# RWKV-7 attention feeding a SoLU expert on one core: carrying the products with r as 64 more columns through carry, drive and solve, and placing full-array runs between runs of 64x64 groups

## The chip, the core and the metric

The kernel runs on one core of one Trainium2 chip. The metric is device time in microseconds for one execution of the whole program, everything from the inputs in DRAM to the output in DRAM. The kernel before the change took 622.96 us (median of three runs: 614.93, 622.96, 625.33). Everything is computed in fp32.

## The reference, cut to what matters

Two blocks follow each other. The first is a recurrence over 768 time steps for 4 batches x 8 heads, each with a 40x40 state; its output of 3072 tokens x 320 goes into the second, a feed-forward block with a softmax-weighted activation (SoLU), a normalisation and a second matrix.

```
state = 0                                           # B=4, H=8, D=40 x D=40
for t in range(768):
    y[:, :, t] = einsum('bhd,bhde->bhe', r_t, state)
    Sa = einsum('bhde,bhe->bhd', state, a_t)
    state = state * w_t[:, :, None, :] - einsum('bhd,bhe->bhde', Sa, b_t)
    state = state + einsum('bhd,bhe->bhde', v_t, k_t)

x = y.transpose(0, 2, 1, 3).reshape(3072, 320)
h = x @ w_in                                        # 320 -> 1024
e = exp(h - max(h));  solu = h * e / (sum(e) + 1e-9)
mu = mean(solu);  var = mean((solu - mu) ** 2)
out = ((solu - mu) / sqrt(var + 1e-6) * g_ln) @ w_out   # 1024 -> 320
```

`moe_w_in`, `moe_w_out` arrive as 64-bit floats (seen as int64) and are narrowed to fp32 on the chip during the first iterations.

## The kernel before, in words

**Chunks.** Time is cut into chunks of 64 steps (C). Two batches are handled together, so there are 24 units of work i = 0..23: pair `bp = i % 2` and chunk `ci = i // 2` (`where_`, L285). Within a chunk the recurrence becomes a few matrix products and the inverse of a unit lower triangular 64x64 matrix per head, here 16 heads of 64 at a time (two batches x eight heads). A unit `(p, q, g, h)` (L257) is one batch p and one head 4q+2g+h. The products of 64x64 (or 40x64) use the tensor engine as four tiles of 64x64, and `in_turn` (L259) orders 16 of them so that the four tiles take turns. Such a group of 16 products is called a group here. All of them go through `mm` (L267), so the profile shows them at L268. Products of the second block use the full 128x128 array.

**Pieces of one iteration.** The main loop (L835 to L905) runs i from -1 to 27. One iteration works on four chunks at once: on chunk i (solve, read out), on i+1 (couple, carry, drive), on i+5 (`j = i + AHEAD`; the keys, `norm`, the inverse) and on m-2 = i-3 and m-3 = i-4 (the second block). In the order of the tensor engine before the change:

- `solved(i)` (L576): 16 products into `pu`, 64 columns (`x0` by `tu`, giving `nuT`, the transposed solution), and 16 into the same buffer with 40 columns (`lu`'s right part). ScalarE copies both out, negated.
- `scores(i+1)` (L530): two groups into `ps`, masked on VectorE into `psi` and the left 64 columns of `lv`. `lv` holds per head 64 columns of masked v-by-r products and 40 columns of v.
- transposes: `stated(i)`, `front(j)`, `front_b(j)`, `decay_turned(j+1)`, eight of them each (`turned`, L350); evicted to `s`, `aT`, `bT`, `ex`.
- `hidden(m-2)` (L673): the second half of `h = x @ w_in` as full-array products with 512 columns (two with 64 rows, two full), with `decay(j+2)`'s product `pcum` between.
- `norm(j)` (L406): one group into `pnt`; ScalarE copies it into `nt`, and POOL writes `nt` to DRAM.
- `answered(i)` (L595): one group into `pl`, `nuT` by `rT`; VectorE masks it into the left 64 columns of `lu`.
- `carried(i+1)` (L548): one group into `px`, `aT` by the state, 40 columns.
- `read(i, True)` (L606): into `pyo`, first `s` by `rT` (64 columns, the state times r), then half of the products `kb` by `lv` and `kb` by `lu` with 104 columns (64 of output, 40 of new state).
- `output(m-3)` (L738): eight full-array products `lnT` by `w2` into `po`, evicted by ScalarE as `osb` (scaled by `rs`) and written out by a DMA on ScalarE's queue.
- `fence` (L272, a drain of the tensor engine), `couple(i+1)` (L479) into `py`, `read(i, False)`, the other half of `pyo`, `driven(i+1)` (L564), the second part of `px`, 40 columns, evicted to `x0`, and `close(i+1)` (L492) into `pz`, evicted into `tu`.
- `leave(i)` (L630): VectorE multiplies the left 64 columns of `pyo` by the decays `ex` into `x`, and SP writes `x` to `xT` by DMA; VectorE adds the right 40 to the state into `tot`, and POOL multiplies by `ex` into the state `st`.
- `attend_r(i+2)` (`pr`), `folded(m-2)` (16 transposes of `e` into `plnT`), `attend_kv(i+2)` (`pkv`), and `hidden(m-1)`, the first two products of the next `h`.

**Other engines.** ScalarE (ACT) does the exponentials, most evictions and, in `spreadof` (L709), the squares for the variance with an accumulator. VectorE (DVE) does the masks, `nmax` (the row maxima of `h`, L690), `weighed` (L700, `e` times `h`) and the inverse. POOL scales keys (`scaled`, L341), multiplies the state, takes the power for `rs`, and issues some DMAs. SP issues most DMAs, in program order.

**The inverse.** The diagonal 32x32 blocks of two chunks together (`GRP` = 2) are inverted on VectorE by `invert` (L435): `nt` is gathered from DRAM into `blk`, then 30 steps of a product (`prod`, L448) and a subtraction (`uu`, L450) follow. The generator is advanced by `some(n)` and `narrow(...)`; `pieces` (L837) says how many steps stand at each place of an iteration: (5, 2, 2, 5) in odd iterations, (6, 2, 2, 6) in even ones. The result goes to DRAM (`uu_dram`, L456, on SP), is read back as `tu` and `uh` by `bring` (L460) at the start of the iterations that come next, and `flip` (L473) transposes `tu`'s blocks on VectorE ahead of `couple`.

**What sets the order.** The kernel is scheduled by hand: each engine executes in the order of the program text, and semaphores are put in where data or buffers demand it. On-chip buffers for matrix products are shared by tag ("A", "B", "C" and "h", each of two banks, one buffer per tag), so a new tile of a tag waits for the readers of the last.

Of the kernel before, what the change touches and what calls it, by code (L numbers as in the profile page):

```python
# [17 lines left out]
P = 128  # L18
C = 64
# [31 lines left out]
def kernel(  # L51
# [32 lines left out]
    small = ctx.enter_context(tc.tile_pool(name="small", bufs=4))  # L84
# [41 lines left out]
    st_t = zeroed(nc.vector, "st", [P, 8, C], NPAIR)  # L126
    tu_t = zeroed(nc.vector, "tu", [P, H, 3 * Q], 2)
    uh_t = zeroed(nc.vector, "uh", [P, 2 * H, Q], 2)
    x0 = zeroed(nc.vector, "x", [P, 2, 4, C], 1, lambda x: x[:, :, :, D:])[0]
# [264 lines left out]
    def masked(dst, t):  # L394
        nc.vector.tensor_tensor(out=dst, in0=t.rearrange("p b (j c) -> p b j c", j=4),  # L395
                                in1=tri.unsqueeze(1).unsqueeze(1).to_broadcast([P, 2, 4, C]), op=ALU.mult)
# [9 lines left out]
    def norm(i):  # L406
        if not ok(i):
            return
        d = st[i]
        t = pair("A", "pnt")  # L410
        for u in in_turn(lambda p, q, g, h: (h, p ^ h)):
            p, q, g, h = u
            j = 2 * q + g
            mm(t[half(p ^ h), h, j * C:j * C + C], keyed(d["bT"], u), keyed(d["aT"], u))
        nt = d["nt"] = tokens("nt", AHEAD)
        nc.scalar.copy(out=nt, in_=t[:, :, 0:256].rearrange("p b (j c) -> p b j c", j=4))  # L416
# [18 lines left out]
    def invert(n):  # L435
# [18 lines left out]
        for y in range(2):  # L454
            queue = nc.sync if n or not y else nc.scalar
            queue.dma_start(out=inverse[n][:, y::2], in_=u[C * y:C * y + C])  # L456
# [22 lines left out]
    def couple(i, tag):  # L479
        if not ok(i):  # L480
            return
        d = st[i]
        t = pair(tag, "py")
        for u in in_turn(lambda p, q, g, h: (p ^ h, p)):
            p, q, g, h = u
            j = 2 * q + g
            x = half(p ^ h)
            mm(t[half(p), h, j * Q:j * Q + Q], d["nt"][x, h, j], d["tu"][x, 4 * h + j, 0:Q])
        nc.scalar.activation(out=wy[:, :, :, 0:Q], in_=t[:, :, 0:4 * Q].rearrange("p h (j c) -> p h j c", j=4),
                             func=AF.Copy, scale=c_("neg_hi"))  # L490

    def close(i):  # L492
# [3 lines left out]
        t = pair("B", "pz")  # L496
        for u in in_turn(lambda p, q, g, h: (p, p ^ h)):
            p, q, g, h = u
            j = 2 * q + g
            mm(t[half(p ^ h), h, j * Q:j * Q + Q], wy[half(p), h, j], d["uh"][half(p), 2 * (4 * h + j) + (p ^ h)])  # L500
# [4 lines left out]
    def attend_kv(i):  # L505
        if not ok(i):
            return
        d = st[i]
        t = pair("B", "pkv")
        k, v = turned(t, 0, d["kb"]), turned(t, 1, v_t[0])  # L510
        d["kT"] = kept("kT", k)
        d["vT"] = kept("vT", v)

    def attend_r(i, tag):
        if not ok(i):
            return
        st[i]["rT"] = kept("rT", turned(pair(tag, "pr"), 0, r_t[0]), 2)

    def stated(i, t, y):
        if not ok(i):  # L520
            return lambda: None
        d = st[i]
        bp, ci = where_(i)
        if not ci:
            return lambda: None
        t = turned(t, y, st_t[bp])
        d["s"] = two.tile([P, 4, P], FP32, tag="s", name="s", bufs=1)
        return lambda: nc.scalar.copy(out=d["s"][0:W2].rearrange("p j (b t) -> p b j t", b=2), in_=t)

    def scores(i):  # L530
        if not ok(i):
            return
# [10 lines left out]
        psi = d["psi"] = tokens("psi", 2)  # L543
        masked(psi, t[:, :, 0:256])
        masked(d["lv"].rearrange("p (q x) c -> p q x c", q=2)[:, :, :, 0:C], t[:, :, 256:])


    def carried(i):  # L548
# [7 lines left out]
        if ci:  # L556
            for u in in_turn(lambda p, q, g, h: (h, p ^ h)):
                p, q, g, h = u
                j = 2 * q + g
                mm(d["px"][half(p ^ h), h, j * D:j * D + D], keyed(d["aT"], u),  # L560
                   st_t[bp][rows(h), 4 * p + 2 * g + q, 0:D], start=(h, p ^ h) not in d["opened"], stop=False)
                d["opened"].add((h, p ^ h))

    def driven(i):  # L564
# [3 lines left out]
        for u in in_turn(lambda p, q, g, h: (p, p ^ h)):  # L568
            p, q, g, h = u
            j = 2 * q + g  # L570
            mm(d["px"][half(p ^ h), h, j * D:j * D + D], d["psi"][half(p), h, j],
               d["lv"][half(p), head(u), C:W2], start=(h, p ^ h) not in d["opened"])
            d["opened"].add((h, p ^ h))
        nc.scalar.copy(out=x0[:, :, :, 0:D], in_=d["px"][:, :, 0:4 * D].rearrange("p h (j d) -> p h j d", j=4))

    def solved(i):  # L576
        if not ok(i):
# [3 lines left out]
        for u in in_turn(lambda p, q, g, h: (p ^ h, q)):  # L581
            p, q, g, h = u
            at, x = (2 * h + g) * C, half(p ^ h)
            mm(t[half(q), p ^ h ^ q, at:at + C], x0[x, h, 2 * q + g], d["tu"][x, 4 * h + 2 * q + g, Q:])
        for u in in_turn(lambda p, q, g, h: (p ^ h, p)):
            p, q, g, h = u
            at, x = 256 + (2 * q + g) * D, half(p ^ h)
            mm(t[half(p), h, at:at + D], d["tu"][x, 4 * h + 2 * q + g, Q:], x0[x, h, 2 * q + g, 0:D])
        nuT = d["nuT"] = tokens("nuT")
        lu = d["lu"] = two.tile([P, H, W2], FP32, tag="lu", name="lu", bufs=1)  # L590
        nc.scalar.mul(out=nuT[0:W2], in_=t[0:W2, :, 0:256].rearrange("p b (j c) -> p b j c", j=4), mul=-1.0)
        nc.scalar.mul(out=lu.rearrange("p (j h) c -> p h j c", h=2)[:, :, :, C:],
                      in_=t[:, :, 256:256 + 4 * D].rearrange("p h (j d) -> p h j d", j=4), mul=-1.0)

    def answered(i):  # L595
# [3 lines left out]
        t = pair("B", "pl")  # L599
        for u in in_turn(lambda p, q, g, h: (q, p)):  # L600
            p, q, g, h = u
            at = (2 * g + h) * C
            mm(t[half(p), q, at:at + C], d["nuT"][rows(q), p ^ h ^ q, 2 * h + g], valued(d["rT"], u))
        masked(d["lu"].rearrange("p (q x) c -> p q x c", q=2)[:, :, :, 0:C], t[:, :, 0:256])

    def read(i, own):  # L606
        if not ok(i):
            return
        d = st[i]
        bp, ci = where_(i)  # L610
        if own:
            d["po"] = pair("A", "pyo")
            d["opened"] = set()
            if ci:
# [321 lines left out]
```

## Time and profile before

| | us |
|---|---|
| three runs | 614.93, 622.96, 625.33 (median 622.96) |
| profiled execution, its own time | 621.36 |
| its span in the trace | 619.5 |
| PE matmuls busy (12,309 of them) | 518.1 |
| PE weight loads busy | 367.3 |
| DVE busy (1,119 instructions) | 404.5 |
| ACT busy (668) | 317.3 |
| POOL busy (441) | 261.6 |
| DVE, the inverse's `prod` and `uu` (720 instructions) | 209.7 |
| PE, `h<-w_in,xT` | 125.3 |
| PE, `po<-w,lnT` | 109.5 |
| 2% of the median | 12.5 |

Mean granted clock of the tensor engine: 0.915. The chain of work that ended last lies on PE for 63% of the span, on DVE for 17%, on "issue" for 8% (time in which the engine waited for nothing that the profile shows), on DMA for 5%, on ACT for 3%.

A row of a timeline reads: start in us from the start of the span, duration in us, engine, line of the code, operation, output tile and input tiles, shape, how many instructions are put together in the row (x8), and in brackets how long the engine stood idle before and what ended that. PEld is the loading of weights into the array, which overlaps PE. SPq, ACTq are DMA issues on the queues of SP and ACT.

### The profile page before, as it was taken

What the parts mean: (1) busy time and instruction counts of PE and PEld (TensorE: products, weight loads), DVE (VectorE), ACT (ScalarE), POOL (GpSimd) and SP (SyncE); (2) the same over time, 40 slices, a digit from 0 to 9 for tenths busy, and PEclk for the clock granted to TensorE, in tenths of its full rate; (3) what the DMA queues carried; (4) which work ended last, traced back from release to release, by engine and by line L of the source; (5) the groups of instructions that cost most, each with busy time, mean ns of one, the idle gap of its engine ahead of it and who ended that gap; (6) DMA issues with size and microseconds to landing.
All of it is one profiled execution on the core that took longest, in us unless ns stands there. A gap on an engine that the chain in (4) does not pass through costs nothing.

```text
span 619.5 us, 28385 instructions
## 1 busy us (share of the span) xinstructions
PE 518.1 (84%) x12309; PEld 367.3 (59%) x12309; DVE 404.5 (65%) x1119; ACT 317.3 (51%) x668; POOL 261.6 (42%) x441
## 2 busy tenths in 40 slices
PE   5443776887889989899889799989899898999993
PEld 3332665665667667666666566757666566756552
DVE  4695889888977858767766658578676575332230
ACT  4534455565556556565555355656554455544332
POOL 3362354275572555444714625625634433122200
PEclk9655656599999999999899989999999999999999
DMA  8986977557545554654654553655523432110100
GB/s 161 158 158 110 192 150 136 110 120 127 91 105 96 114 119 98 121 110 93 125 90 81 121 91 72 126 96 102 107 56 73 92 62 51 33 34 26 27 19 21
DMA packets 213907, 60.03 MB, mean 97 GB/s; under 512 B 199120, under 2 KB 208952, under 8 KB 213784
## 3 DMA queue, kind: packets, MB, share of 16 engines
q1 hardware_dynamic: 195512, 33.78, 33.2%
q0 software_dynamic: 11568, 19.78, 13.5%
q10 hardware_dynamic: 6704, 4.67, 2.8%
q8 instruction: 97, 1.59, 1.1%
q14 instruction: 26, 0.21, 0.1%
HBM read 40.10 MB, written 13.37 MB: 86 GB/s over the span
## 4 chain that ended last, share of the span: by engine, by line
PE 63%; DVE 17%; issue 8%; DMA 5%; ACT 3%; POOL 1%; SPq 0%; ACTq 0%; DVEq 0%; POOLq 0%
PE h L268 18%; PE po L745 12%; DVE uu L450 5%; PE pyo L268 5%; DVE prod L448 5%; PE pu L268 4%; PE ps L268 4%; PE px L268 3%; PE py L268 2%; PE plnT L731 2%; PE pst L355 2%; PE pcum L336 2%; PE pkv L355 2%; PE pz L268 2%; DMA blk<-nt_dram 2%
## 5 line engine op out<-in xcount | busy, mean ns | idle before, releaser
L268 PE MATMUL h<-w_in,xT 128*128 128x512 f32 (+1 forms) x288 | 125.3, 625 | 0.1
L448 DVE TENSOR_TENSOR prod<-blk,uu 128x30 f32<-128x30 f32 (+4 forms) x360 | 104.7, 291 | 29.7 <-DMA blk<-nt_dram 19.0
L450 DVE TENSOR_TENSOR uu<-uu,prod 128x30 f32<-128x30 f32 (+4 forms) x360 | 105.0, 292 | 12.4
L745 PE MATMUL po<-w,lnT 128*128 128x320 f32 x384 | 109.5, 438 | 1.8 <-ACT lnT L735 1.8
L745 PEld LDWEIGHTS po<-w,lnT 128*128 128x128 f32 x384 | 71.2, 190 | 32.6 <-ACT lnT L735 1.9
L268 PEld LDWEIGHTS h<-w_in,xT 128*128 128x128 f32 (+1 forms) x288 | 41.0, 191 | 43.0 <-issue 38.4
L690 DVE TENSOR_REDUCE nmax<-h 128x1 f32<-128x1024 f32 x24 | 29.4, 1224 | 47.3 <-PE h L268 47.3
L721 POOL TENSOR_TENSOR rs<-var,mhalf 128x1 f32<-128x1 f32 x24 | 13.5, 564 | 100.5 <-ACT var L720 99.9
L421 POOL DMA_DIRECT2D nt_dram<-nt x20 | 18.6, 930 | 85.8 <-ACT nt L416 51.7
L432 POOL DMA_DIRECT2D blk<-nt_dram x46 | 36.8, 806 | 30.1 <-DMA nt_dram<-nt 26.6
L670 POOL DMA_DIRECT2D xT<-x x96 | 48.6, 511 | 0.0
L639 DVE TENSOR_TENSOR x<-pyo,ex 104x256 f32<-104x256 f32 x48 | 18.1, 419 | 46.6 <-PE pyo L268 43.9
L658 POOL TENSOR_TENSOR st<-tot,ex 104x160 f32<-104x160 f32 x44 | 24.2, 567 | 51.3 <-DVE tot L654 51.0
L698 ACT ACTIVATE e<-h,nmax 128x1024 f32<-128x1024 f32 x24 | 26.7, 1114 | 32.1 <-DVE nmax L690 30.1
L336 PE MATMUL pcum<-lw,cst 128*128 128x320 f32 x48 | 23.5, 579 | 22.4 <-ACT lw L327 21.5
L719 ACT ACTIVATE h<-e,mu 128x1024 f32<-128x1024 f32 x24 | 26.8, 1118 | 19.8 <-DVE e L706 19.8
L395 DVE TENSOR_TENSOR psi<-ps,cst 128x512 f32<-128x512 f32 x24 | 16.5, 687 | 28.1 <-PE ps L268 27.9
L291 POOL DMA_DIRECT2D raw_r<-in_r_dram x48 | 34.1, 713 | 0.0
L747 ACT ACTIVATE osb<-po,rs 128x320 f32<-128x320 f32 x24 | 12.6, 525 | 41.6 <-PE po L745 39.9
L268 PE MATMUL pyo<-lu,kb 64*64 64x104 f32 x768 | 29.4, 262 | 5.4 <-DVE lu L395 3.1
L706 DVE SCALAR_TENSOR_TENSOR e<-h,e 128x1024 f32<-128x1024 f32 x24 | 29.3, 1219 | 5.8 <-ACT e L698 5.8
L268 PE MATMUL py<-tu,nt 64*64 64x32 f32 x768 | 17.7, 230 | 17.3 <-DVE tu L477 11.3
(136 smaller groups left out, 1101.1 us busy)
## 6 DMA issues: line engine op xcount, KB each, us to landing
blk<-nt_dram POOLq DMA_DIRECT2D x46, 128.0 KB, 4.6
nt_dram<-nt POOLq DMA_DIRECT2D x20, 256.0 KB, 3.8
raw_w<-in_w_dram SPq DMA_DIRECT2D x48, 80.0 KB
a<-in_a_dram SPq DMA_DIRECT2D x48, 80.0 KB
raw_r<-in_r_dram POOLq DMA_DIRECT2D x48, 80.0 KB, 4.0
lv<-in_v_dram SPq DMA_DIRECT2D x48, 80.0 KB
out_dram<-osb ACTq DMA_DIRECT2D x24, 160.0 KB
raw_b<-in_b_dram SPq DMA_DIRECT2D x44, 80.0 KB
```

The source lines that it names most:

```text
L268: nc.tensor.matmul(o, lhsT=lhsT, rhs=rhs, start=start, stop=stop, skip_group_check=True)
L291: queue.dma_start(out=x[half(p), :, 0:D], in_=ap[2 * bp + p, :, ci * C:(ci + 1) * C, :].rearrange("h t d -> t h d"))
L336: nc.tensor.matmul(t, lhsT=c_("cum"), rhs=d["lw"], start=True, stop=True)
L432: queue.dma_start(out=nb[home:home + Q], in_=blocks[n][:, Q * e:Q * e + Q, Q * e:Q * e + Q])
L448: nc.vector.tensor_tensor(out=t, in0=nb[:, j:j + 1, j + 1:Q].to_broadcast([P, n_c, m]), in1=u[:, 0:n_c, j:j + 1].to_broadcast([P, n_c, m]) ...
L450: nc.vector.tensor_tensor(out=u[:, 0:n_c, j + 1:Q], in0=u[:, 0:n_c, j + 1:Q], in1=t, op=ALU.subtract)
L670: nc.gpsimd.dma_start(out=xT[to:to + Q, 2], in_=x[at + P - 3 * D:at + D, 2])
L690: nc.vector.tensor_reduce(out=nmax, in_=d["h"], axis=AX.X, op=ALU.max, negate=True)
L698: nc.scalar.activation(out=e, in_=d["h"], func=AF.Exp, bias=d["nmax"], accum_out=d["esum"])
L706: nc.vector.scalar_tensor_tensor(out=d["e"], in0=d["h"], scalar=1.0 / DFF, in1=d["e"], op0=ALU.mult, op1=ALU.mult, accum_out=d["mu"])
L719: nc.scalar.activation(out=d["h"], in_=d["e"], func=AF.Square, scale=-float(DFF), bias=d["mu"], accum_out=sq)
L745: nc.tensor.matmul(t, lhsT=d["lnT"][:, f, :], rhs=w2[:, f, :], start=f == 0, stop=f == NF - 1)
```

## The change

It does the following.

- The state's tile `st` gets a second plane of 64 columns. A new group `stated_r(i+1)` makes the state times r first (`s` by `rT` into `psr`), and ScalarE puts it into plane 0; plane 1 is the state as before. `carried` then runs with both planes, 128 columns, `driven` with the 104 columns of `lv` (in place of its right 40), `x0` holds 104 columns per head, negated at its eviction, and `solved` makes one group with 104 columns in place of two. Its left 64 columns are masked straight from `pu` into `lu`. `nuT`, `answered` and the group `pl` are gone, and so is `pyo<-rT,s`: `leave` adds plane 0 to `pyo`'s left columns instead.
- `leave` adds both parts on VectorE into a `tot` of 104 columns, and the multiplication by the decays into `x` is on POOL (it was on VectorE).
- `read(i)` is one run, and it stands ahead of `output`, with `leave` behind it. `output` is in two halves of four products: one behind `read`, one behind `norm`.
- `couple` and `norm` share one buffer and follow each other; `norm` moves from behind `highest` to behind `couple`, so that the writing of `nt`, and on every second iteration the start of the next inverse, move too. The drain ahead of `couple` is gone. `flip` moves up to just behind `highest`, `spreadof` behind `norm`, `weighed` behind `leave`.
- `stated` now works for i+1, and the order and the buffers of the transposes change: `pst` takes `stated` and `front_b`, "A" takes `front` and `decay_turned`. `attend_kv` evicts with one copy for k and v, `folded` with one in place of two, and the evictions of the three are put behind all their transposes. `hidden` runs (2,0), (2,1) and then, behind the transposes, (0,1), (1,1) without `pcum` between.
- The inverse's steps per iteration: (0, 2, 2, 10) in odd iterations, (3, 2, 2, 9) in even ones.

```diff
-    st_t = zeroed(nc.vector, "st", [P, 8, C], NPAIR)
+    st_t = zeroed(nc.vector, "st", [P, 2, 8, C], NPAIR)
...
-    x0 = zeroed(nc.vector, "x", [P, 2, 4, C], 1, lambda x: x[:, :, :, D:])[0]
+    x0 = const.tile([P, 2, 4, W2], FP32, name="x0")
...
+    def stated_r(i):
...
+        t = pair("C", "psr")
+        for u in in_turn(lambda p, q, g, h: (q, h)):
+            p, q, g, h = u
+            at = (2 * p + g) * C
+            mm(t[half(h), q, at:at + C], d["s"][rows(q), 2 * p + g, h * C:h * C + C], valued(d["rT"], u))
+        nc.scalar.copy(out=state_of(i)[:, 0].rearrange("p (x q) c -> p q x c", q=2), in_=by_units(t[:, :, 0:256]))
...
-                mm(d["px"][half(p ^ h), h, j * D:j * D + D], keyed(d["aT"], u),
-                   st_t[bp][rows(h), 4 * p + 2 * g + q, 0:D], start=(h, p ^ h) not in d["opened"], stop=False)
+                mm(d["px"][half(p ^ h), h, j * P:j * P + P], keyed(d["aT"], u),
+                   state_of(i)[rows(h), :, 4 * p + 2 * g + q], start=(h, p ^ h) not in d["opened"], stop=False)
...
-            mm(d["px"][half(p ^ h), h, j * D:j * D + D], d["psi"][half(p), h, j],
-               d["lv"][half(p), head(u), C:W2], start=(h, p ^ h) not in d["opened"])
+            mm(d["px"][half(p ^ h), h, j * P:j * P + W2], d["psi"][half(p), h, j],
+               d["lv"][half(p), head(u)], start=(h, p ^ h) not in d["opened"])
...
-        nc.scalar.copy(out=x0[:, :, :, 0:D], in_=d["px"][:, :, 0:4 * D].rearrange("p h (j d) -> p h j d", j=4))
+        nc.scalar.mul(out=x0, in_=d["px"].rearrange("p h (j d) -> p h j d", j=4)[:, :, :, 0:W2], mul=-1.0)
...
-        for u in in_turn(lambda p, q, g, h: (p ^ h, q)):
-            p, q, g, h = u
-            at, x = (2 * h + g) * C, half(p ^ h)
-            mm(t[half(q), p ^ h ^ q, at:at + C], x0[x, h, 2 * q + g], d["tu"][x, 4 * h + 2 * q + g, Q:])
...
+            at, x = (2 * q + g) * W2, half(p ^ h)
+            mm(t[half(p), h, at:at + W2], d["tu"][x, 4 * p + 2 * q + g, Q:], x0[x, h, 2 * q + g])
...
+        nc.scalar.copy(out=o[:, :, :, C:], in_=y[:, :, :, C:])
+        masked(o[:, :, :, 0:C], y[:, :, :, 0:C])
...
-    def answered(i):
...
+            for x, part in enumerate((slice(0, C), slice(C, W2))):
+                nc.vector.tensor_tensor(out=by_b(tot)[:, :, :, part], in0=y[:, :, :, part],
+                                        in1=by_b(state_of(i)[:, x])[:, :, :, 0:part.stop - part.start], op=ALU.add)
...
-            nc.vector.tensor_tensor(out=x[0:W2, 2 * q:2 * q + 2].rearrange("p g (b t) -> p b g t", b=2),
-                                    in0=y[:, q, :, 0:C].rearrange("p (b g) c -> p b g c", b=2),
-                                    in1=ex[:, :, 2 * q:2 * q + 2, 0:C], op=ALU.mult)
+            nc.gpsimd.tensor_tensor(out=x[0:W2, 2 * q:2 * q + 2].rearrange("p g (b t) -> p b g t", b=2),
+                                    in0=by_q(tot, q)[:, :, :, 0:C], in1=ex[:, :, 2 * q:2 * q + 2, 0:C], op=ALU.mult)
...
-        pieces = shares.get(i, (5, 2, 2, 5) if i % GRP else (6, 2, 2, 6))
+        pieces = shares.get(i, (0, 2, 2, 10) if i % GRP else (3, 2, 2, 9))
```

The new order of the main loop, behind `solved(i)` and `scores(i+1)`:

```
hidden(m - 2, ((2, 0), (2, 1)))
tc_, ta = pair("C", "pst"), pair("A", "pa")
for evict in [stated(i + 1, tc_, 0), front_b(j, tc_, 1), front(j, ta, 0), mask_values, decay_turned(j + 1, ta, 1)]:
    evict()
hidden(m - 2, ((0, 1), (1, 1)))
decay(j + 2); stated_r(i + 1); narrow(some_weights[1], pieces[1])
highest(m - 2); flip(i + 1); scaled(j + 1); left(i - 1)
exped(m - 2); by_value(i + 2); read(i); some(pieces[2])
output(m - 3, 0); leave(i); weighed(m - 2); carried(i + 1)
coupled = couple(i + 1); norm(j, coupled)          # and begin_inverse in every second iteration
spreadof(m - 2); output(m - 3, 1); narrow(some_weights[2], pieces[3], ...)
close(i + 1); driven(i + 1)
keys_out, fold_out, r_out = attend_kv(i + 2), folded(m - 2), attend_r(i + 2, "C")
for evict in [fold_out, keys_out, r_out]:
    evict()
hidden(m - 1, ((0, 0), (1, 0)))
```

## The prediction, made before the changed kernel ran

> **What bounds the kernel now.** I read the page's busy shares first, then the clock and the instruction queue, then the timeline of the tensor engine through one iteration after another.
>
> ```profile
> PE 518.1 (84%) x12309; PEld 367.3 (59%) x12309; DVE 404.5 (65%) x1119; ACT 317.3 (51%) x668; POOL 261.6 (42%) x441
> ...
> PEclk9655656599999999999899989999999999999999
> ...
> q8 instruction: 97, 1.59, 1.1%
> ```
>
> The tensor engine (PE) is the busiest; its clock is full after the first fifth except for two dips. Queue q8 moved 97 packets of 1.59 MB in all, 16 KB each. PE's 24,618 loads and matmuls make 254 per packet. So q8 brings PE's own instructions, 256 at a time.
>
> I date iterations by the first matmul into `pu`: 160.26 us at i=4, 361.05 at i=13, 380.47 at i=14, 486.94 at i=19, 562.30 at i=23. From i=4 to 18 all work runs: 15 iterations of 21.78 us. But i=13 took 19.42, with no gap in it. The 2.36 us between are gaps of this kind:
>
> ```profile
> 219.79 0.39 PE L355 MATMUL pkv<-cst,kb 64*104 64x64 f32 x8
> 220.02 0.33 PE L355 MATMUL pkv<-cst,v 64*104 64x64 f32 x5
> 221.40 0.32 PE L355 MATMUL pkv<-cst,v 64*104 64x64 f32 x3 [1.06 <-issue]
> 221.65 1.98 PE L268 MATMUL h<-w_in,xT 128*128 128x512 f32 x4
> ```
>
> The engine stops inside a run of equal transposes and waits for nothing that a semaphore shows. Numbering PE's records from the first, every such stop from 160 us on stands behind number 256k+192, and a q8 packet comes just before it ends. At these boundaries PE loses 30.9 us from i=4 to 18, 3.7 us from i=19 to 22, and 5.7 us between 60 and 160 us. Two long stops (2.74 us at 303.1, 3.87 at 350.3) are followed by 3.4 and 6.8 us at half clock, where `h<-w_in` takes 3.40 in place of 1.98 us; worked from such rows that is 4.5 us more. Together 39.1 us after 160, on the path because nothing else holds PE there.
>
> When does a boundary stop PE? From one boundary to the first instruction behind the next, the stopped ones take 3.4 to 4.5 us (181.26 to 185.18, 258.78 to 263.24), three late ones 7.8 to 10.8. If the 256 instructions between take longer than that, nothing is lost. An fp32 product is two loads and two matmuls, so 16 products of 64x64 are 64 instructions in 0.44 to 0.52 us, while eight full-array products for `po` are 32 in 4.5 us. The dense run from `pnt` to the first `pyo` holds 320 instructions in 2.8 us, that from `py` to `pkv` 304 in 3.1: a block inside lasts about 2 us, and PE waits for the other two.
>
> **PE work, part by part, per iteration**, in start-to-start times. Out: `pu`'s groups of 64 and 40 columns (0.51+0.44), `pl` (0.46), the 40-column `px` groups (0.44 each), the drain in front of `py` (0.22): 2.51. In: `pu` with 104 columns and drive with 104 (16 products of 104 took 0.36+0.38 in `pyo`: 0.74 each), carry with 128 (0.74 x 128/104 = 0.91): 2.39. `psr` replaces `pyo<-rT,s` at 0.50. Turns between 64x64 and full-array work go from three each way to five: the last group ahead of such a run shows 0.46 against 0.36 us, the first behind it 0.52 against 0.46 to 0.49, so 2 x 0.15 = 0.30. Net +0.18 (-0.1 to +0.4): 3.4 us over the 19 iterations.
>
> The Trainium skill speaks against these turns: "TensorEngine Tiling (Array Packing)", section "Key Properties", says that a change of tiling mode drains the engine. If a drain costs a whole matmul row (262 ns in `pyo`), four more turns are an estimated 1.05 us per iteration, and the sum below would be some 14 us higher; the rows above show a tenth of a microsecond.
>
> **Fetch.** The new iteration has 908 such instructions for 1,036, in runs of at most 208 between full-array pieces: `psr`+`pyo` 192 in 2.1 us, `po`'s first half 16 in 2.25, carry to `norm` 192 in 2.0, `po`'s second half, `pz` to `pr` 208 in 2.1, `h` 8 in 1.9, `pu`+`ps` 192 in 1.8, `h` 8 in 1.0. Sliding a window of 256 over this gives at least 3.65 us (from `pu`), elsewhere 4.3 to 7.3. So ordinary stops go, save perhaps 0.15 us per iteration (2.3 in all). Late fetches can still hurt; the three and their slow clock cost 8.1+4.5, and I keep half, 6.3. Gain 39.1-2.3-6.3 = 30.5 us (22 to 39).
>
> "Runtime: NRT & Kernel Launch" of the skill, section "Instruction fetch mechanics", also has 16 KB blocks, but calls the cost of crossing one mostly hidden. By that rule this gain is nil, and the change would end near 652 us; the trace shows 35 us of stops after 160 us.
>
> **What is late next: ScalarE.** After `norm`'s last product (E), ACT must finish a fixed row before PE may go on.
>
> ```profile
> 321.54 1.12 ACT L719 ACTIVATE h<-e,mu 128x1024 f32<-128x1024 f32 x1 [0.70 <-DVE e L706]
> 322.59 0.19 ACT L719 ACTIVATION_READ_ACCUMULATOR h<-e,mu 128x1 f32 x1
> 322.81 0.29 ACT L720 ACTIVATE var<-sq,c 128x1 f32<-128x1 f32 x1
> 326.68 0.53 ACT L747 ACTIVATE osb<-po,rs 128x320 f32<-128x320 f32 x1 [3.57 <-PE po L745]
> 327.23 0.53 ACTq L748 DMA_DIRECT2D out_dram<-osb  x1
> 327.81 0.47 ACT L489 ACTIVATE wy<-py,cst 128x256 f32<-128x256 f32 x1 [0.60 <-PE py L268]
> ```
>
> Today `wy` comes after `osb` and its DMA, and `nt` early. The new order is `wy` 0.47, `nt` 0.58, `c2` 0.29, Square 1.12+0.19, `var` 0.29, `osb` 0.53, its DMA 0.53, `tu` 0.38, `x0`. `x0` grows from 320 to 832 elements: between 0.42 (320) and 1.11 (1024), 0.87. With 0.27 from a group's last issue to its reader that is 5.5 us by durations, 5.0 if neighbours overlap by 0.1 as `s`, `bT`, `ex` do (starts 0.48 apart, 0.59 long). `pr` takes `px`'s buffer and must wait for `x0`; PE's own work from E to `pr` (half `po` 2.25, `pz` 0.48, `px` 0.74, `pkv` 0.46, `plnT` 0.49) is 4.4. So PE waits 0.6 to 1.1 us; I take 0.65, neighbours overlapping. In the four iterations without `norm`, 0.3. Sum 11.0 us (9 to 18). `nuT` (0.59) leaves and `psr`'s copy (0.59) comes, both beside `h`.
>
> **VectorE and POOL.** The two masks' waits (`lu` on `pl`) go: `lu` now reads `pu`, 5 us ahead of its use. `x`, `tot`: 2x0.42+2x0.31 becomes 0.68+0.48, as `x` moves to POOL, 2 x 0.77 (between 0.57 at 160 and 0.90 at 320 elements). That is not free for DVE:
>
> ```profile
> 243.19 1.28 DVE L448 TENSOR_TENSOR prod<-blk,uu 128x126 f32<-128x126 f32 x1
> ...
> 243.41 0.90 POOL L348 TENSOR_TENSOR kb<-raw_b,inv 128x320 f32<-128x320 f32 x1
> ...
> 244.24 0.95 POOL L348 TENSOR_TENSOR kb<-raw_k,inv 128x320 f32<-128x320 f32 x1
> 244.50 0.83 DVE L450 TENSOR_TENSOR uu<-uu,prod 128x126 f32<-128x126 f32 x1
> ```
>
> Two steps that take 0.57 us alone take 2.1 beside POOL. So `x` costs DVE about 1.35 us, against 0.3 saved; DVE's 13.7 to 16.9 us per iteration (i=13, i=4) stay under 20.
>
> **The way of the inverse, and SP's queue.** With the pieces above, `norm` ends 12.6 us behind `pu`. On DVE `nmax` starts at 6.6, `flip` at 7.8 (now 10.4), two steps and `tot` follow to 10.6, `weighed` to 11.9; the inverse's last step, nine small ones (4.5) and up to 1.6 of POOL's share later, ends at 16.4 to 18 (now 13.6), in every second iteration (i even). What hangs on it:
>
> ```profile
> 258.31 1.27 SPq L456 DMA_DIRECT2D uu_dram<-uu  x2
> 260.56 0.81 SPq L645 DMA_DIRECT2D xT<-x  x1
> 261.48 2.40 SPq L646 DMA_DIRECT2D xT<-x  x1
> ...
> 268.21 0.83 SPq L469 DMA_DIRECT2D tu<-uu_dram  x2
> ...
> 277.67 1.27 SPq L291 DMA_DIRECT2D raw_k<-in_k_dram  x2
> ```
>
> SP reads `tu` back 8.6 us after it began to write `uu` (nine cases, 7.0 to 9.9), and `uh`, `lv`, `raw_w`, `raw_b`, `a`, `raw_k` stand behind that wait: 10.7 us of issuing, to 278.94. Nobody needs them soon. But `leave` moves up to mid-iteration, and its four `xT` writes stand behind all this; and ACT's `out_dram` DMA, whose place is now ahead of `tu` and `x0`, reuses a completion semaphore whose last user, in the built program of the odd iterations, is the second `xT` write (in the even ones `raw_k`, which is early there; before, both were loads far earlier). So ACT waits for SP. In numbers, from the odd iteration's `pu` at 20.3 (19.42+0.18+0.65): last step 17, round trip 7.0 (its kindest row, as no `xT` writes come between any more), `tu` issued at 24.0, that is 3.7; `raw_k` issued by 14.4; second `xT` write 0.9 later; landed 2.6 later (median of `xT`): 17.9. `out_dram`'s turn is at 15.9 (`norm`'s end 12.6, 0.27, and five rows of ACT less overlaps). Wait 2.0 us, all of it PE's, for `x0` and `pr` come behind. Eight odd iterations (5 to 19): 16 us. Bounds: `xT` in time, 0; last step at 18 and 9.9, 5.9 x 8 = 47. `flip` itself is late only if round trip and landing exceed 11.1 us from 17. On POOL, `x`, `nt_dram` and `blk` push back `rs`, `raw_r`, `kb` and `xT`: `kb` and `xT` are wanted a whole iteration later, `rs` by the next `osb`. The start up to 160 us, where DVE's steps and half clock set the pace, I leave alone (-5 to +5), as I do the tail.
>
> **Sum**, against the profiled execution's 621.36 us (span 619.5, 0.3% under the median 622.96): -30.5+3.4+11.0+16.0 = -0.1. I forecast 621: fetch gains 30 us, and ACT and SP take them back.
>
> **Rivals.** (a) Faster: `xT` lands in time, as where the last step ends at 15 us or the round trip takes 5: 621.4-16.1 = 605; with ACT's smaller 9 and all 39 of the fetch 595, with a wait of 0.6 us 610. For it: two microseconds decide it, out of a chain of 38. Against: no row of the nine is under 7.0. (b) Slower: SP's wait at the mean round trip of 8.6 and a last step at 17.5: `out_dram` waits 4.1 us, eight times 33: 638. It is beyond 2% from 3.75 us on, `tu` issued 5.5 us behind the odd `pu`. For it: 8.6 is the mean, and `blk`'s gather (256.88) still leaves with the write. Against: four `xT` writes less in between. (c) Fetch stops stay, since the crossing costs whatever runs there: the gain is 0 to 10, the total 640 or more. Against: no stop in i=13, whose instructions are the same.
>
> **Numbers.** Forecast 0.36, its own range 611 to 633; (a) 0.33, (b) 0.24, (c) 0.07. Three runs of this kernel spread by 1.7%, so about 2% (12.5 us) can be told. Faster than 610.5: (a) and 0.01 of the forecast, 0.34. Slower than 635.4: (c), 0.24 of (b) and 0.01 of the forecast, 0.32. Within 2%: 0.34. The range 599 to 643 leaves out the ends of (a), (b) and (c).
>
> **What would show it.** Right: PE's stops behind 256k+192 shrink from 2.06 to under 0.5 us per iteration; full iterations alternate, even ones near 20.3 us, odd ones 2 to 3 longer; in the odd ones ACT idles between `osb` and `out_dram`, released by a DMA. Wrong: iterations of one length near 20.3 (a); odd ones 4 us longer (b); stops of 1 to 2 us at the boundaries (c); matmul rows near the turns longer by 0.2 us.

## The result, and the profile after

The changed kernel takes 631.22 us (median of 17 runs, 625.84 to 638.21) against 624.03 us for the one before (17 runs): a ratio of 1.0147, 95% interval 1.0102 to 1.0192, some 9 us slower. The ratio is taken over the executions that lie within 1.5% of each kernel's fastest. The forecast was 621 us, no change; the time lies inside the range of 599 to 643, on its slow side, but the interval shows a small loss where none was forecast. The profiled execution took 626.38 us (span 624.6), at the low end of its runs, so the spans below show 5.1 us of the difference.

The page after, the same lines as before (busy us and instructions, clock in 40 slices, instruction queue):

```profile
PE 529.5 (85%) x10773; PEld 370.2 (59%) x10773; DVE 403.8 (65%) x1072; ACT 317.1 (51%) x618; POOL 290.3 (46%) x489
...
PEclk9555767689789999899899998998999989999997
...
q8 instruction: 85, 1.39, 1.0%
```

There are an eighth fewer matmuls, and PE is busy for longer: the clock row has more dips than before (mean 0.894 against 0.915), and a slow matmul counts as busy. Queue q8 fits the reading that it brings PE's instructions: with the drains and semaphore instructions in PE's stream the traces hold 24,916 of PE's records before and 21,799 after, that is 97.3 and 85.2 blocks of 256, for 97 and 85 packets. The stops behind instruction 256k+192 are all but gone: 40.2 us before, 3.0 us after, summed over the span by the same numbering. So the main gain came. Where did it go? The first matmul into `pu` dates each iteration:

| | before | after |
|---|---|---|
| first `pu` (i=0) to i=5, us | 112.1 | 123.9 |
| i=5 to 18, 14 iterations | 305.8 | 300.1 |
| of these, i=6, 8, 10, 12 | 21.2, 21.4, 23.7, 27.1 | 19.8, 19.8, 19.9, 19.8 |
| and i=7, 9, 11, 13, 15 | 21.1, 21.2, 22.9, 19.4, 22.2 | 24.9, 23.6, 25.3, 23.2, 24.1 |
| i=19 to 22 | 75.4 | 75.2 |
| i=23 to the end of the span | 57.3 | 56.8 |

Two losses stand against the gain: five odd iterations that are 3 to 6 us longer than their neighbours, and 11.8 us in the first five. The first is seen in iteration 7 (`pu` at 232.21). PE's timeline:

```profile
248.96 0.39 PE L355 MATMUL pkv<-cst,v 64*104 64x64 f32 x8
252.72 0.94 PE L738 MATMUL plnT<-cst,e 64*128 64x64 f32 x16 [3.37 <-ACT tu L513]
253.49 0.67 PE L355 MATMUL pr<-cst,r 64*104 64x64 f32 x8
254.09 3.11 PE L268 MATMUL h<-w_in,xT 128*128 128x512 f32 x4
```

`plnT` takes the buffer of `pz`, and ScalarE's copy `tu` frees it. That copy is late. The timeline of ScalarE:

```profile
247.82 0.53 ACT L756 ACTIVATE osb<-po,rs 128x320 f32<-128x320 f32 x1
251.72 0.54 ACTq L757 DMA_DIRECT2D out_dram<-osb  x1
252.29 0.37 ACT L513 COPY tu<-pz 128x256 f32<-128x256 f32 x1 [3.94 <-DMA xT<-x]
252.56 0.87 ACT L606 ACTIVATE x<-px 128x832 f32<-128x832 f32 x1
```

`pz` is done at 248 us, so ScalarE could copy `tu` from then on. But `out_dram` stands in front, and it is issued only 3.37 us after `osb` is ready. ScalarE waits there for the semaphore that `out_dram` and the second `xT` write share; the `xT` write, which has no data in common with `out_dram`, releases it. And SP's queue, from the write of the inverse in iteration 6 on:

```profile
228.37 1.43 SPq L468 DMA_DIRECT2D uu_dram<-uu  x2
237.09 0.81 SPq L481 DMA_DIRECT2D tu<-uu_dram  x2
...
245.14 2.20 SPq L291 DMA_DIRECT2D raw_k<-in_k_dram  x2
247.66 0.80 SPq L660 DMA_DIRECT2D xT<-x  x1
248.56 0.79 SPq L661 DMA_DIRECT2D xT<-x  x1
```

SP waits for the write to land (8.72 us), then issues 10.25 us of reads that stood behind, then `xT`, whose `x` POOL had finished at 244.8. The second `xT` write has landed 3.1 us after its issue, and `out_dram` goes 0.1 us later. This is the chain that the prediction drew; it costs 3.37, 2.10, 4.11, 2.12 and 3.10 us on ScalarE in iterations 7, 9, 11, 13 and 15, together 14.8 us. The four matmuls of `h` above take 3.11 us in place of 1.98: the clock falls to half for 3.41 us behind each of these waits and adds up to 1.7 us. The five iterations are 21.8 us longer than five of 19.9. A table by stretches of the clock (the column behind POOL is the granted clock) in iteration 9, whose wait ended at 295.97:

```profile
297.50:300.58 3.08, 3.08 (x4) 0.67 (x2) 1.85 (x7) 2.01 (x4) 1.76 (x4) 0.50 0.56 114
300.58:302.00 1.42, 1.42 (x73) 1.42 (x76) 0.00 (x0) 0.33 (x1) 0.00 (x0) 0.93 0.47 93
```

By the profile PE stood idle there for 1.90 us; 2.11 us lie between the starts of the last matmul ahead of the wait and the first behind it. The Trainium skill, "TensorE: Matmul & The Clock Gate", section "HAM oscillation — how this bites in real kernels", warns of idle gaps of more than about 3.4 us; in this trace 1.90 us are already followed by 3 us at half clock, and the measurement decides. The length of the pause alone does not settle it, though. In the kernel before, a stop of 2.12 us was followed by full clock, at which four matmuls of `h` take 1.98 us:

```profile
484.71 0.32 PE L355 MATMUL pkv<-cst,v 64*104 64x64 f32 x4 [2.12 <-issue]
484.96 1.98 PE L268 MATMUL h<-w_in,xT 128*128 128x512 f32 x4
```

The second loss is at the start. PE's waits in front of `py` in iterations 0 to 3, before:

```profile
85.44 1.08 PE L268 MATMUL py<-tu,nt 64*64 64x32 f32 x32 [2.63 <-DVE tu L477]
...
104.45 1.08 PE L268 MATMUL py<-tu,nt 64*64 64x32 f32 x32 [1.64 <-DVE tu L477]
...
128.23 0.67 PE L268 MATMUL py<-tu,nt 64*64 64x32 f32 x32 [1.01 <-DVE tu L477]
...
151.64 0.67 PE L268 MATMUL py<-tu,nt 64*64 64x32 f32 x32 [1.68 <-DVE uu L450]
```

After, with VectorE's rows ahead of the first of them:

```profile
83.94 0.23 DVE L460 TENSOR_TENSOR prod<-blk,uu 128x65 f32<-128x65 f32 x1
84.20 0.23 DVE L462 TENSOR_TENSOR uu<-uu,prod 128x65 f32<-128x65 f32 x1
84.34 1.02 DVE L650 COPY tot<-pyo 104x832 f32<-104x832 f32 x1
...
85.42 1.08 PE L268 MATMUL py<-tu,nt 64*64 64x32 f32 x32 [6.02 <-DVE tot L650]
...
106.96 1.08 PE L268 MATMUL py<-tu,nt 64*64 64x32 f32 x32 [2.61 <-DVE tot L650]
...
131.19 0.67 PE L268 MATMUL py<-tu,nt 64*64 64x32 f32 x32 [2.37 <-DVE tot L647]
...
155.33 1.08 PE L268 MATMUL py<-tu,nt 64*64 64x32 f32 x32 [3.69 <-DVE tot L647]
```

Iterations 0 to 3 together, and iteration 4, by engine (busy us: PE, weight loads, DVE, ACT, POOL; then the clock). Before:

```profile
68.97:160.26 91.29, 69.52 (x1839) 53.79 (x1838) 80.04 (x222) 52.26 (x113) 44.13 (x70) 0.77 0.68 130
160.26:181.03 20.77, 19.47 (x519) 14.04 (x519) 16.89 (x45) 12.39 (x27) 11.17 (x19) 1.00 0.55 103
```

After:

```profile
68.63:167.89 99.26, 70.13 (x1624) 55.23 (x1622) 82.07 (x217) 53.01 (x108) 54.02 (x82) 0.76 0.72 126
167.89:192.49 24.60, 23.04 (x454) 16.06 (x455) 14.37 (x35) 11.97 (x24) 8.12 (x13) 0.86 0.26 53
```

`couple` now shares a buffer with `norm` that `pyo` had, so it waits until `pyo` is read into `tot`, and this stands on VectorE behind the steps of the inverse. The waits of `py` in these four iterations grow from 7.0 to 14.7 us, and the four iterations from 91.3 to 99.3: almost all of the 8 us is this wait. VectorE is busy for 80 to 82 us in both. The fifth iteration, 3.8 us longer, has a dip of the clock behind its own wait for `tot` (0.86); in a later run, at full clock, it took 21.4 us.

### The profile page after: what moved, and what is told of

Its sections match the earlier page's. It is cut to its first block, busy times and chain, and to the rows that moved or that the text cites. A ratio compares the mean times of both kernels' runs of the same rounds, so it can differ in the third digit from the quotient of the medians.

```text
span 624.6 us, 25176 instructions
## 1 busy us (share of the span) xinstructions
PE 529.5 (85%) x10773; PEld 370.2 (59%) x10773; DVE 403.8 (65%) x1072; ACT 317.1 (51%) x618; POOL 290.3 (46%) x489
## 4 chain that ended last, share of the span: by engine, by line
PE 50%; DMA 15%; ACT 11%; DVE 10%; issue 6%; POOL 4%; SPq 2%; ACTq 1%; POOLq 0%; DVEq 0%
PE h L268 17%; PE po L752 9%; DMA blk<-nt_dram 4%; DMA nt_dram<-nt 4%; PE py L268 4%; PE pyo L268 3%; ACT h L726 3%; DVE uu L462 3%; PE px L268 3%; PE pu L268 3%; PE ps L268 3%; DMA xT<-x 2%; DVE prod L460 2%; POOL blk L444 2%; PE psr L268 2%
## 5 line engine op out<-in xcount | busy, mean ns | idle before, releaser
L268 PE MATMUL h<-w_in,xT 128*128 128x512 f32 (+1 forms) x288 | 128.8, 652 | 0.3
L752 PE MATMUL po<-w,lnT 128*128 128x320 f32 x384 | 120.1, 460 | 2.5 <-ACT lnT L741 2.5
L655 POOL TENSOR_TENSOR x<-tot,ex 104x256 f32<-104x256 f32 x48 | 33.0, 704 | 159.5 <-DVE tot L647 135.1
L752 PEld LDWEIGHTS po<-w,lnT 128*128 128x128 f32 x384 | 72.5, 197 | 33.6 <-issue 4.9
L395 DVE TENSOR_TENSOR lu<-pu,cst 128x512 f32<-128x512 f32 x24 | 16.6, 690 | 88.6 <-ACT lu L620 88.6
L444 POOL DMA_DIRECT2D blk<-nt_dram x46 | 36.2, 794 | 24.3 <-DMA nt_dram<-nt 21.8
L697 DVE TENSOR_REDUCE nmax<-h 128x1 f32<-128x1024 f32 x24 | 29.3, 1220 | 26.3 <-PE h L268 26.3
L501 ACT ACTIVATE wy<-py,cst 128x256 f32<-128x256 f32 x24 | 11.4, 474 | 65.1 <-PE py L268 65.1
L268 PE MATMUL py<-tu,nt 64*64 64x32 f32 x768 | 17.3, 232 | 23.2 <-DVE tot L647 9.8
L548 ACT COPY s<-pst 104x512 f32<-104x512 f32 x22 | 12.9, 586 | 41.0 <-PE pst L355 41.0
L382 DVE TENSOR_TENSOR aT<-pa,ex 104x512 f32<-104x512 f32 x24 | 16.6, 690 | 24.6 <-PE pa L355 18.2
L433 POOL DMA_DIRECT2D nt_dram<-nt x20 | 19.2, 959 | 27.1 <-ACT c L725 26.5
L268 PEld LDWEIGHTS py<-tu,nt 64*64 64x64 f32 x768 | 16.3, 151 | 25.7 <-issue 15.5
```

The source lines that it names most:

```text
L268: nc.tensor.matmul(o, lhsT=lhsT, rhs=rhs, start=start, stop=stop, skip_group_check=True)
L444: queue.dma_start(out=nb[home:home + Q], in_=blocks[n][:, Q * e:Q * e + Q, Q * e:Q * e + Q])
L655: nc.gpsimd.tensor_tensor(out=x[0:W2, 2 * q:2 * q + 2].rearrange("p g (b t) -> p b g t", b=2), in0=by_q(tot, q)[:, :, :, 0:C], in1=ex[:, : ...
L697: nc.vector.tensor_reduce(out=nmax, in_=d["h"], axis=AX.X, op=ALU.max, negate=True)
L752: nc.tensor.matmul(t, lhsT=d["lnT"][:, f, :], rhs=w2[:, f, :], start=f == 0, stop=f == NF - 1)
```

## The experiments

Times are medians, ratios are to the kernel before, measured on the same chip.

**out_dram on SP.** What is taken away is ScalarE's place behind SP's late queue, and with it the 0.53 us that the issue took on ScalarE in every iteration; the DMA, the loads and the inverse stay.

```diff
-        nc.scalar.dma_start(out=out.rearrange(...)[...], in_=osb)      # in output
+        nc.sync.dma_start(out=out.rearrange(...)[...], in_=osb)        # behind output, thus behind xT
```

> The changed kernel, with the DMA of the result (out_dram) issued on SP behind the xT writes in place of ACT. Theory A (in odd iterations SP's queue stands behind the read-back of the inverse, xT goes late, and ACT, whose out_dram waits for that xT write, holds back tu and x0): the 2.1 to 4.1 us waits of plnT for ACT in iterations 7, 9, 11, 13, 15 go, with the half clock behind them; odd iterations fall from 23.2-25.4 us to 20-22, the total by 9 to 20 us against the changed kernel, about 611 to 622. Theory B (the inverse is late by itself: flip and tot on DVE would stop PE at the same place): the wait moves to py, the total stays within 4 us of the changed kernel. Theory C (the loss lies with x on POOL, which slows DVE): within 3 us as well, and py waits no longer than now.

Measured: 609.16 us, ratio 0.9806 (0.9740 to 0.9873), 22 us under the changed kernel and 14 under the one before. ScalarE in iteration 9 of this run (`pu` at 275.48):

```profile
291.34 0.51 ACT L756 ACTIVATE osb<-po,rs 128x320 f32<-128x320 f32 x1
291.78 0.37 ACT L513 COPY tu<-pz 128x256 f32<-128x256 f32 x1
292.53 0.86 ACT L606 ACTIVATE x<-px 128x832 f32<-128x832 f32 x1 [0.37 <-PE px L268]
```

`tu` follows `osb` at once, and the iteration takes 20.24 us; no wait of `plnT` for ACT is left. Theory A holds for the waits and the total, with a little more gain than its range. For the length of the odd iterations it holds in part: 7 to 15 take 22.9, 20.2, 20.2, 25.0 and 21.4 us, 11.5 us less than in the changed kernel. The two profiles differ by 15.2 us in all; 4.6 of these lie from i=19 on, where ScalarE did not wait for `xT` before, so not all of the gain is this wait. B and C, as the main cause, fall. What is left of B shows in iterations 7 and 15, where `py` waits 1.4 and 1.6 us for `tot`, and most in iteration 13. VectorE's timeline there:

```profile
364.44 1.22 DVE L697 TENSOR_REDUCE nmax<-h 128x1 f32<-128x1024 f32 x1
368.02 0.45 DVE L489 STREAM_TRANSPOSE tu<-tu 128x256 f32<-128x256 f32 x1 [2.36 <-DMA tu<-uu_dram]
```

`flip` waits for the read-back of the inverse, `tot` stands behind `flip`, and `py` behind `tot` (2.20 us, then a dip of the clock).

**The read-back out of the way altogether.** In addition `bring` goes behind the loads of `lv` and `raw_w`, and `flip` behind `leave`.

```diff
-        if i >= 1:
-            bring(i + 1)
         if i >= 0:
             load_values(i + 2)
...
             load_keys(j + 3, "w")
+        if i >= 1:
+            bring(i + 1)
         load_keys(j + 2, "bak")
...
-        flip(i + 1)
         scaled(j + 1)
...
         leave(i)
+        flip(i + 1)
         weighed(m - 2)
```

> As the run before, and bring stands behind the loads of lv and raw_w on SP (so only b, a, k are behind the wait for the inverse), and flip stands behind leave's additions on VectorE. Theory A: nothing of the round trip of the inverse is left on the way of xT, x0 or tot; odd iterations equal even ones, 19.8 to 20.3 us; the total falls by 20 to 30 us against the changed kernel, to 600 to 611, below the kernel before. Theory B (DVE's own work per iteration is the next bound): 612 to 622, py waiting for tot in most iterations. Theory C (x on POOL): no better than the run before.

Measured: 609.52 us, ratio 0.9801 (0.9740 to 0.9863): within A's range, and no better than the run before. Its iterations 8 to 17 take 19.6 to 20.8 us, odd and even alike, close to what A said. But iteration 7 takes 22.7 us, and the first `pu` to i=5 takes 124.8 against 123.6: `flip`, put behind `tot`, makes `py` wait for it in the first four iterations (18.4 us), where VectorE is full.

**A later inverse.** A dose of the suspected cause: `uu` written later by two steps.

```diff
-        pieces = shares.get(i, (0, 2, 2, 10) if i % GRP else (3, 2, 2, 9))
+        pieces = shares.get(i, (0, 2, 2, 8) if i % GRP else (3, 2, 2, 11))
```

> The changed kernel with two steps of the inverse moved from the end of the odd iterations to the end of the even ones (pieces (0,2,2,8) and (3,2,2,11)), so that uu is written some 1.0 to 1.2 us later in each even iteration. Theory A: ACT's wait for xT grows by as much in each odd iteration from 5 to 19, in all 7 to 12 us more than the changed kernel. Theory B or C (the odd iterations are long from DVE's own load in them, or from POOL): two steps fewer at the end of the odd iterations, so no change or some 2 to 6 us less.

Measured: 636.48 us, ratio 1.0244 (1.0173 to 1.0314), 5 us over the changed kernel by the medians, a little under A's range, and 8.8 by the spans of the two profiles, within it. The intervals of the two ratios overlap a little, so the size of the difference is uncertain; B and C forecast none or the other sign. `uu` goes out 17.3 us behind the even `pu` in place of 16.0, and iterations 7, 9, 11, 13 and 15 take 129.7 us in place of 121.3. ScalarE in iteration 7:

```profile
249.30 0.53 ACT L756 ACTIVATE osb<-po,rs 128x320 f32<-128x320 f32 x1
253.91 0.55 ACTq L757 DMA_DIRECT2D out_dram<-osb  x1
254.50 0.37 ACT L513 COPY tu<-pz 128x256 f32<-128x256 f32 x1 [4.67 <-DMA xT<-x]
```

The wait is 4.08 us, 0.7 more than with the earlier inverse, and in iteration 9 it is 4.06, 2.0 more. In 11 and 15 it does not grow and in 13 it falls to 0.97, so over all odd iterations it grows by only 2 us. In 13 and 15 `py` waits 1.7 and 1.8 us for `tot` instead, behind a `flip` that is late too; the clock's dips make up the rest. A later inverse lengthens the odd iterations, then, but only in 7 and 9 through the link that A named.

**The kernel before with output in halves.** One part of the change alone, which spaces the dense runs.

```diff
-        output(m - 3)
+        output(m - 3, 0)          # in front of read(i, True)
         read(i, True)
...
         read(i, False)
+        output(m - 3, 1)
```

> The kernel before, with one part of the change alone: output's eight products in two halves, one in front of read(own half), one behind read(other half), so that the two dense runs of 64x64 groups (320 and 304 instructions) become shorter than 256. Theory A (PE waits for the instruction fetch where 256 instructions take under 3.7 us): stops behind instruction 256k+192 fall from 39 us in all to under 20; PE waits new for osb (pz takes its buffer) and for lu, 0.5 to 1 us each per iteration, so the time lies between 610 and 640. Theory B (the stops have another cause, tied to the iteration's length or to DMA traffic): stops of 30 us and more remain.

Measured: 620.09 us, ratio 0.9982 (0.9943 to 1.0022): no change. The stops at the boundaries fall from 40.2 to 12.8 us, as A said. In their place PE waits for `lu`'s mask in front of `po` (17 times, 9.2 us in all), 8 us longer for this mask than before, and 3 us longer for `uu` and `tu` in front of `py`. So spacing does remove the stops, but in the old order the time does not fall. The new waits on VectorE account for some 11 of the 27 us; the rest lies in pieces too short for the profile's list of waits (iteration 10 takes 20.8 us without a stop, 19.4 in the undisturbed i=13 before), and what they are stays open.

**The first iterations, steps moved.** In iterations -1 to 4 the steps ahead of `tot` go behind it, with `out_dram` on SP.

```diff
-    shares = {-1: (0, 2, 3, 9), 0: (4, 5, 3, 4), 1: (0, 6, 4, 5), 2: (4, 4, 3, 4), 3: (0, 5, 4, 4), 4: (6, 1, 4, 6)}
+    shares = {-1: (0, 2, 0, 12), 0: (4, 2, 0, 10), 1: (0, 4, 0, 11), 2: (4, 2, 0, 9), 3: (0, 2, 0, 11), 4: (6, 1, 0, 10)}
```

> The changed kernel with out_dram on SP (609.2 us) and, in iterations -1 to 4 alone, the inverse's steps that stand ahead of leave's additions put behind them (shares (0,2,0,12), (4,2,0,10), (0,4,0,11), (4,2,0,9), (0,2,0,11), (6,1,0,10)). From the first pu to i=5 the changed kernel takes 123.9 us, the one before 112.1. Theory A (these 11.8 us are lost because couple now shares its buffer with pyo and so stands behind the additions into tot, which on a full VectorE stand behind steps of the inverse): py's waits for tot up to i=4 fall from 20 us to under 10, and the total to 600 to 606. Theory B (VectorE is full there, and whatever is put later is waited for elsewhere): the first five iterations stay at 120 us or more, the total at 606 to 613.

Measured: 609.44 us, ratio 0.9769 (0.9669 to 0.9869). Iteration 0 falls from 24.6 to 19.9 us and the fifth from 24.6 to 19.6, but i=2 and i=3 grow from 25.1 and 28.1 to 29.3 and 32.0; the first five take 123.0 us, 0.6 less. `py` waits less for `tot`; `pa` waits 12 us for `lu`'s mask, behind the steps that now stand there. Theory B.

**x back on VectorE**, with `out_dram` on SP.

```diff
-            nc.gpsimd.tensor_tensor(out=x[0:W2, 2 * q:2 * q + 2]..., op=ALU.mult)
+            nc.vector.tensor_tensor(out=x[0:W2, 2 * q:2 * q + 2]..., op=ALU.mult)
```

> The changed kernel with out_dram on SP (609.2 us), and with the multiplication into x back on VectorE, where the kernel before has it. Theory A (x on POOL costs VectorE shared time and puts it behind POOL's other work, and this is part of the loss): 600 to 607. Theory B (VectorE is the nearest bound once the waits are gone, and two multiplications of 0.42 us more in front of weighed hold back ScalarE's squares): 610 to 620.

Measured: 611.76 us, ratio 0.9803 (0.9719 to 0.9887): no difference that can be told from the 609.2 with `x` on POOL. The first five iterations take 124.6 us here too. Where `x` is computed is not where the loss lies.

**bring later, flip later from i=5 on**, with `out_dram` on SP and `bring` as in the second run.

```diff
+        if i < 5:
+            flip(i + 1)           # behind highest, as in the changed kernel
...
         leave(i)
+        if i >= 5:
+            flip(i + 1)
```

> out_dram on SP, bring behind the loads of lv and raw_w, and flip behind the additions from iteration 5 on only (before it, flip stays in its early place). The run with flip late from the start had its first pu to i=5 3 us longer than now and iterations 7 to 18 shorter. Theory A (flip late is good where the read-back sets its time, and bad where VectorE is full): 600 to 607. Theory B (the two runs differ by fetches and clock dips alone): 607 to 612.

> The kernel without that edit, on the same chip, so that the two differ by it alone: 605 to 611 us.

Measured: 610.14 us (0.9769, 0.9686 to 0.9852), and in a second set of runs 608.66 us (0.9797, 0.9746 to 0.9849). Iterations 7 to 18 take 241.2 and 241.3 us in the two profiles against 249.0 with `out_dram` on SP alone, so that part of A holds twice; iteration 19, at 22 us against 19.9, and the first five, at 123.0 and 127.4 against 123.6, give much of it back. As a total it can't be told from the run with one edit. (What the expectation says of the run with `flip` late from the start is too much: up to i=5 it was 1.2 us longer, not 3.) The four versions with `out_dram` on SP, `bring` where it was or later, lie at 608.7 to 610.1 us and are all some 2% faster than the kernel before: the intervals leave out 1, but not a gain a little under 2%.

**output undivided**, with `out_dram` on SP.

```diff
-        output(m - 3, 0)          # behind read
...
+        output(m - 3, 0)
         output(m - 3, 1)          # behind norm
```

> The changed kernel with out_dram on SP (609.2 us), and output's eight products undivided behind norm, so that psr to norm is one dense run of 384 instructions. Theory A (spacing keeps the instruction fetch ahead): stops behind 256k+192 come back, 10 to 30 us in all; the total 620 to 640. Theory B (the new order has so few instructions that 908 per iteration are fetched in time in any order; the halves matter only as cover for ScalarE): stops stay under 5 us; PE's waits are then for ACT and DVE, and the total is 609 to 630.

Measured: 634.95 us, ratio 1.0181 (1.0076 to 1.0285), 26 us over the divided one by the medians, 23 by the ratios. The stops stay at 2.4 us, as B said, and yet the time lies in A's range. PE in iteration 9:

```profile
287.05 0.66 PE L268 MATMUL px<-st,aT 40*64 40x128 f32 x12 [0.35 <-issue]
289.54 0.67 PE L268 MATMUL py<-tu,nt 64*64 64x32 f32 x32 [1.84 <-DVE tot L647]
290.00 0.70 PE L268 MATMUL py<-aT,bT 40*64 40x64 f32 x32
```

`py` comes right behind `px` and waits for `tot` (21 times, 36.4 us in all, against 8 times and 15.3 us in the divided run). That wait may be what gives the fetch its time; whether the dense run would stop without it this run can't tell. What it shows is that the half of `output` between `read` and `carried` covers VectorE's additions: without it `py`'s waits grow by 21 us.

**An own buffer for the first three iterations**, on top of the best order.

```diff
-            shared[i] = pair("A", "py")
+            shared[i] = pair("h" if 1 <= i <= 3 else "A", "py")
```

> As the run with out_dram on SP, bring later and flip later from iteration 5 on (605.4 us in the profiled execution, median 610.1), with one edit: couple and norm of the first three iterations take the free buffer h in place of pyo's. Theory A (the first iterations are long because couple waits for the additions into tot, which free pyo's buffer behind VectorE's steps): the waits of py for tot up to i=2, 13 us, go or fall below 4, and the first pu to i=5 falls from 123.0 us to 113 to 119; the total to 597 to 605. Theory B (VectorE's own work sets the first iterations whatever PE does; the wait moves to the masks, to flip or to weighed): the first five iterations stay within 3 us of 123, the total within 3 us of 606 to 610.

Measured: 612.71 us, ratio 0.9838 (0.9785 to 0.9891), not better than 608.66 without it. `py` no longer waits for `tot` in iterations 0 to 2 (10.9 us without the edit), but in the first two it waits 5.3 us for `flip`. Iteration 0 falls from 24.5 to 21.1 us, and i=3 grows from 29.8 to 35.5; the first five take 130.7 us against 127.4. VectorE's timeline there, and PE's `py`:

```profile
153.81 0.68 DVE L454 TENSOR_TENSOR uu<-blk,above 64x512 f32<-64x512 f32 x1 [7.29 <-DMA blk<-nt_dram]
157.11 0.19 DVE L460 TENSOR_TENSOR prod<-blk,uu 128x30 f32<-128x30 f32 x1 [2.46 <-DMA blk<-nt_dram]
```

```profile
164.32 1.08 PE L268 MATMUL py<-tu,nt 64*64 64x32 f32 x32 [11.23 <-DVE tot L647]
```

The steps of the next inverse stand in front of `flip` and `tot` and wait 9.75 us for the gather of `blk`. So at the start the wait for `tot` is not one cause that can be cut out: freed in one iteration it returns in another, on VectorE's order of steps. Which of the changed kernel's moves (the later `norm` and with it the later `blk`, `tot` in front of `couple`, the early `flip`) accounts for the 8 us of the first four iterations stays open.

## Why the prediction was right and wrong

**Fetch: right, undersized.** The stops fell from 40.2 to 3.0 us; expected were 2.06 us per full iteration to under 0.5, measured is 0.07. The block model held, also in the kernel before with only the spacing added, though there the time did not fall with the stops. By the rule of the Trainium skill that the prediction weighed ("Runtime: NRT & Kernel Launch", section "Instruction fetch mechanics"), there was nothing to gain; both traces speak against it.

**PE work: right.** Even iterations take 19.8 to 19.9 us; 19.42 + 0.18 = 19.6 was expected without ScalarE's term.

**ScalarE behind `norm`: too dear.** I took 0.65 us per full iteration, 11.0 in all. The even iterations leave 0.2 to 0.3 us for it. In iteration 8 `pr` starts 0.76 us behind `plnT`, where `plnT` took 0.49 before; that is the only trace of the wait.

**SP's queue and `out_dram`: the mechanism right in each link, the size not.** Measured in iteration 7, from the even and odd `pu`: `uu` written at 16.0 (I took 17), round trip 8.7 (7.0), `tu` issued at 4.9 (3.7), `raw_k` done at 15.1 (14.4), second `xT` write at 16.4 (15.3), landed 3.1 later (2.6), `osb` ready at 16.1 (15.9): a wait of 3.4 us in place of 2.0. The wrong choice was "round trip 7.0 (its kindest row, as no `xT` writes come between any more)": without these writes the five long iterations still have 8.6 to 9.3. Nor did I count the clock behind such a wait. Three of the eight odd iterations escape it: 5, after a round trip of 4.45 us, and 17 and 19, where no keys are left to load (`raw_k` goes out last at 436.4). The five cost 21.8 us over 19.9 each; the term was 16 for eight. Rival (b), with the mean round trip, gave 4.1 us and 638; it had the better round trip, but a last step 1.5 us too late.

**The step that failed most: "The start up to 160 us, where DVE's steps and half clock set the pace, I leave alone (-5 to +5)".** It cost 11.8 us up to i=5: 8.0 in the first four iterations, where `py`'s waits grow by 7.7, and 3.8 in the fifth. That VectorE sets the pace there was right, and was the reason to look: `couple` moved into the buffer of `pyo` and so behind `tot`, a wait that the change adds, and I did not ask what is queued on VectorE in front of `tot` in the iterations where that engine is full. Taken off the profile, this loss would leave the changed kernel 7 us faster than the one before. But the runs that moved the steps or gave `couple` another buffer did not win it back, so which part of the change has to be undone for that stays open.

Together, in the profile: 14 iterations at 19.9 us would have been 27 us less than before; the long ones took 22 back, the start 12. That the time still came within 2% of the forecast is in part luck. SP's queue and the start cost some 18 us more than their terms; the stops with their slow clock (some 7 us) and ScalarE (some 6 us) cost less than theirs, and hid most of it.

## What to carry to other kernels

A DMA issue in an engine's instruction stream can be a wait like any other: here it stood behind a transfer of another queue with which it shared a semaphore and no data. Follow it through each queue in order, in every parity of the loop, and put it on a queue whose delay nobody on the critical path shares; here one moved line was worth some 22 us. When a wait is priced from rows that spread, the kindest row needs a reason that the trace shows, and a wait that the change adds has to be priced first where its engine is busiest, at the start of the run.

## What the runs showed of the hardware

The tensor engine can lose its full clock after shorter pauses than I expected: 1.90 us of idling in iteration 9 were followed by half clock, and so were 1.56 us in iteration 4. But 2.12 us in the kernel before, at 484.71, were not, nor the same 1.56 us in iteration 4 of the run with `flip` late from i=5 on. So the length of the pause is not all that counts; what else does, these runs don't show. Behind the five waits of iterations 7 to 15 the half clock lasted 3.41 us each time. A wait on PE can therefore cost more than it lasts: the one in iteration 9 lengthened its iteration by 3.8 us against its neighbours, and the 3.37 us in iteration 7 by 5.1.
